# Two attention blocks in one kernel: a two-step projection that may spread over two slots, with a reordered start

## The chip, the cores and the metric

The kernel runs on one core of one Trainium2 chip. The metric is the device time of one execution in microseconds (us), the median of several runs. "Full exponential" below means one ScalarE (ACT) instruction over 128 x 1536 elements.

## The reference

Two multi-head attention blocks, A with full and B with windowed causal attention, each on its own input of 2048 x 512, 32 heads of 16. The results are laid side by side.

```python
def _A_ref(x, wqkv, wo):
    B, S, D = x.shape                      # 1, 2048, 512
    H = 32
    Dh = D // H                            # 16
    qkv = ((x @ wqkv).reshape(B, S, 3, H, Dh)) ...   # to q, k, v by head
    scores = jnp.einsum("bhqd,bhkd->bhqk", q, k) * (Dh ** -0.5)
    p = _softmax(scores, axis=-1)
    o = jnp.einsum("bhqk,bhkd->bhqd", p, v)
    return (... o ...).reshape(B, S, D) @ wo

# _B_ref is the same with W = 256 and, before the softmax:
    mask = (idx[:, None] - idx[None, :] >= 0) & (idx[:, None] - idx[None, :] < W)
    scores = jnp.where(mask[None, None], scores, -1e9)

return jnp.concatenate([a, b], axis=-1)
```

Everything is bf16 at the inputs and the output.

## The kernel before

The kernel is a software pipeline of 731 slots. A slot has three jobs; a job is one head's scores for 128 keys and up to 512 queries. For each slot PE multiplies the scores into three PSUM banks (the tile sps, of which there are two), ACT takes the exponential of all three banks in one instruction (pT), and PE multiplies pT by the values (op). Two slots ahead, the next scores are already being made.

Around this, smaller work is filled in, one step at a time: projections of keys, values and queries and the output product. Each has two steps of two 128x512 products, accumulated in a single bank called ms, which DVE then copies out. A part of the exponentials of block A is not done by ACT but by a polynomial on DVE (steps "d"): one score product into the same bank ms, a copy by DVE, and three DVE operations for every two of them.

Where PE has little else to do in a slot, it multiplies unread products into the scores' bank ahead of the scores; the scores overwrite them. `whole` counts what was filled in during the slot.

```python
    def busy(self, bank, n):
        for _ in range(n):
            self.nc.tensor.matmul(bank, lhsT=self.ident[:], rhs=self.junk, start=True,
                                  stop=True)                                  # line 156

    def scores(self, slot):
        sps = self.ps.tile([P, SLOT, 512], FP32, name="sps", tag="sps", bufs=2)
        for b, jb in enumerate(slot["jobs"]):
            ...
            if b == 0 and jb.inst == 0:                # inst 0 is block A, 1 is block B
                self.busy(sps[:, 0, :], 2 - self.whole)
            for kt, q0, q1, o in jb.subs:
                self.nc.tensor.matmul(sps[:, b, o:o + q1 - q0], ...)          # line 572
        ...                                            # masks of block B, line 581
```

A projection is a pair of steps. The bank is taken in the first and given back in the second:

```python
    def pair(self, first, second):
        def f():
            self.open = self.bank()
            first(self.open[:])                        # products of chunks 0 and 1, line 252
        def g():
            bank, self.open = self.open, None
            self.closed = self.slot
            second(bank[:])                            # chunks 2 and 3, then DVE's copy
        return [f, g]
```

The step of the polynomial, cut to its bank:

```python
        def step(jb):
            ...
            b = self.bank()
            ... nc.tensor.matmul(b[:, o:o + q1 - q0], ...)                    # line 628
            nc.vector.tensor_copy(out=y[:, half, :], in_=b[:])                # line 631
            self.closed = self.last_poly = self.slot   # next one two slots later at best
            ...                                        # three DVE operations, lines 642 to 652
```

A fill is refused when the bank was given back in this very slot, or when DVE would not have freed it:

```python
    def fill(self, s, tasks, done):
        if self.open is None:
            if self.closed == s or not self.by(self.freed, 0.9):
                return False
            self.cur = next((t for t in tasks if t["nb"] <= s and t["after"] <= done
                             and t["ok"]()), None)
            if self.cur is None:
                return False
        t = self.cur
        kind = t["name"][0]
        self.whole += (kind in "kqop") * 2 + (kind in "dv")
        t["steps"].pop(0)()
        ...
```

The loop pays every step from a credit, which grows by the steps that are due per slot:

```python
        for n in range(2):
            self.whole = n - 1
            self.scores(slots[n])
        self.whole = 2
        for s, sl in enumerate(slots):
            self.slot = s
            self.exps(sl)                              # line 599
            ...
            if s + 2 < len(slots):
                self.scores(slots[s + 2])
            ...
            self.values()                              # line 691
            ...
            credit = min(credit + min(self.rate(s, tasks), 2.5), 3.0)
            poly_credit = min(poly_credit + self.rate(s, polys), 3.0)
            self.whole = 0
            ...                                        # a guard product, if the bank is free
            full = s + 2 < len(slots) and all(jb.blocks for jb in slots[s + 2]["jobs"])
            if (poly_credit >= (2.5 if full else 1.0) and self.open is None
                    and self.fill(s, polys, done)):
                poly_credit -= 1.0
            must = self.open is not None
            while ((credit >= (CROWD if full else 1.0) or must)      # CROWD is 3.0
                   and self.fill(s, tasks, done)):
                credit -= 1.0
                must = self.open is not None and not full
                if full:
                    break
```

The start multiplies the first four value tiles, nine heads wide, before the first scores:

```python
        nv = 4
        vb = self.ps.tile([P, SLOT, 512], FP32, name="sps", tag="sps", bufs=2)
        for t in range(nv):
            bank = vb[:, t, :] if t < SLOT else tile_("op", 1)[:]
            self.v_mm(0, t, bank, range(NC), (0, HV))
            self.v_evac(0, t, bank, nc.scalar.copy, (0, HV))
            if t == 0:
                self.pad_guard(0, mq)                  # finishes the first queries, on PE and DVE
```

Of the kernel before, what the change touches and what calls it, by code (L numbers as in the profile page):

```python
# [25 lines left out]
NC = D // P  # L26
NPASS = S // 512
NKT = S // P
SLOT = 3
# [12 lines left out]
HV = 9  # L42
# [72 lines left out]
class _Kernel:  # L115
# [443 lines left out]
# [3 lines that stand above are left out]
            r = slice(32 * jb.j, 32 * jb.j + KR)  # L562
            qT = self.qT[jb.inst, jb.p, jb.g // 2]
            gg = jb.g % 2
            assert jb.key != (0, 0, 1) or self.padq_done
            if b == 0 and jb.inst == 0:

                self.busy(sps[:, 0, :], 2 - self.whole)
            for kt, q0, q1, o in jb.subs:
                kT, k0 = self.kT[jb.inst, jb.g // 2, kt // 4]  # L570
                k0 += (kt % 4) * P
                self.nc.tensor.matmul(sps[:, b, o:o + q1 - q0],  # L572
                                      lhsT=kT[r, gg, k0:k0 + P],
                                      rhs=qT[r, gg, q0:q1], start=(o == jb.subs[0][3]),
                                      stop=not jb.blocks, tile_position=(32 * jb.j, 0),
                                      skip_group_check=True)
        for b, jb in enumerate(slot["jobs"]):
            for kind, o in jb.blocks:
                m = self.mask[:, "fd".index(kind[0]):"fd".index(kind[-1]) + 1, :]
                m = m.rearrange("p a n -> p (a n)")  # L580
                self.nc.tensor.matmul(sps[:, b, o:o + P * len(kind)], lhsT=self.ident[:],  # L581
                                      rhs=m, start=False, stop=True, skip_group_check=True)
        slot["sps"] = sps
# [223 lines left out]
    def start(self):  # L807


        nc = self.nc  # L810
        x = self.t[0]["x"].rearrange("(c k p) d -> p c k d", p=P, k=4)
        xs = [self.tile([P, 2, 4, D], BF16, "kTa", NPAIR) for _ in range(2)]
        load = lambda c, h, eng: eng.dma_start(xs[c // 2][:, c % 2, 2 * h:2 * h + 2],
                                               x[:, c, 2 * h:2 * h + 2])
        load(0, 0, nc.sync)
        load(0, 1, nc.scalar)
        self.load_w(0, 1, nc.sync, (0, P))
        self.load_w(0, 0, nc.scalar, (0, P))
        warm = self.consts.tile([1, 1], FP32, name="warm")
        nc.vector.memset(warm[:], 0.0)  # L820
        nc.scalar.activation(out=warm[:], in_=warm[:], func=ACT.Exp)
        for c in range(1, NPASS):
            for h, eng in enumerate((nc.sync, nc.scalar)):
                load(c, h, eng)
        self.load_w(0, 2, nc.sync)
        self.load_w(0, 1, nc.scalar, (P, D))
        self.load_w(0, 0, nc.sync, (P, D))
        self.constants()
        for gg in range(2):
            for n in (1, 0):  # L830
                self.pad_w(n, gg)
        self.padmax = self.consts.tile([P, 2, NPASS], FP32, name="padmax")
        self.k_begin(0, 0, 0)
        tile_ = lambda tag, bufs: self.ps.tile([P, 512], FP32, name=tag, tag=tag, bufs=bufs)
        big = {}

        def turn(c):
            for h in range(2):
                t = self.ps.tile([P, SLOT, 512], FP32, name="sps", tag="sps", bufs=2)
                tb = big[c, h] = t[:, 0, :].bitcast(BF16).rearrange("p (d n) -> p d n", d=2)  # L840
                for d in range(2):
                    for k in range(4):
                        nc.tensor.transpose(tb[:, d, k * P:(k + 1) * P],
                                            xs[c // 2][:, c % 2, k, (2 * h + d) * P:
                                                       (2 * h + d + 1) * P], self.ident[:])

        def keep(c):
            xT = self.tile([P, NC, 512], BF16, "xT", XRING)
            self.xT[0, c] = xT
            for h in range(2):  # L850
                copy = nc.vector.tensor_copy if h else nc.scalar.copy
                copy(out=xT[:, 2 * h:2 * h + 2, :], in_=big[c, h])

        def keys(c):
            b = self.bank() if c == 2 else tile_("op", 1)
            self.pad_mm(1, 0, c, b[:], range(NC))
            self.pad_k_evac(0, c, b[:])
        for i, n in ((0, NKT), (1, VRING_B)):
            for t in range(n):
                self.v_begin(i, t)  # L860
        b = self.bank()
        for _ in range(36):
            nc.tensor.matmul(b[:, 0:P], lhsT=self.ident[:], rhs=self.ident[:], start=True,
                             stop=True)
        turn(0)
        keep(0)
        turn(1)
        keep(1)
        keys(0)
        b = self.bank()  # L870
        self.pad_mm(0, 0, 0, b[:], range(NC))
        mq = self.pad_q_evac(0, b[:])
        for c in range(2, NPASS):
            turn(c)
            keep(c)
            keys(c - 1)
        keys(NPASS - 1)
        nv = 4
        vb = self.ps.tile([P, SLOT, 512], FP32, name="sps", tag="sps", bufs=2)
        for t in range(nv):  # L880
            bank = vb[:, t, :] if t < SLOT else tile_("op", 1)[:]
            self.v_mm(0, t, bank, range(NC), (0, HV))
            self.v_evac(0, t, bank, nc.scalar.copy, (0, HV))
            if t == 0:
                self.pad_guard(0, mq)
        self.qT[0, 0, 0] = self.padq
        return [("v", 0, t, 0) for t in range(nv)] + [("k", 0, 0), ("q", 0, 0, 0)]

# [127 lines left out]
    def run(self):  # L1016
# [6 lines left out]
        tasks = self.tasks = [t for t in tasks if t["name"][0] != "d"]  # L1023
        credit = poly_credit = 0.0
        for n in range(2):
            self.whole = n - 1
            self.scores(slots[n])
        self.whole = 2
        for s, sl in enumerate(slots):
            self.slot = s  # L1030
            self.exps(sl)
            if s == 2:
                self.more_constants()
                self.load_wo(0)
            if self.dq and self.by(self.vec, 0.6):
                self.queued(1.22, at=0)
                self.dq.pop(0)()
            if s + 2 < len(slots):
                self.scores(slots[s + 2])
            elif s + 1 == len(slots):  # L1040
                self.mid, finish = self.last_out(0, NPASS - 1)
            self.values()
            due = [x for x in self.later if x[0] <= s]
            self.later = [x for x in self.later if x[0] > s]
            for _, f in due:
# [4 lines that stand above are left out]
            if (self.guards and self.guards[0][0] <= s and self.open is None  # L1050
                    and self.by(self.freed, 0.9)):
                self.guards.pop(0)[1]()
                self.closed = s
                self.whole = 1
# [5 lines that stand above are left out]
            while ((credit >= (CROWD if full else 1.0) or must)  # L1060
                   and self.fill(s, tasks, done)):
                credit -= 1.0
                must = self.open is not None and not full
                if full:
                    break
        while self.pend:
# [58 lines left out]
```

## Time and profile before

| | before |
|---|---|
| time, median of 3 runs | 1043.58 us (1042.92 to 1048.24) |
| span of the profiled execution | 1041.2 us |
| ACT busy | 998.4 us, 96% |
| PE busy | 942.3 us, 90% |
| DVE busy | 802.5 us, 77% |
| unread products (line 156) | 735 |
| products of polynomial steps (line 628) | 244 |
| granted clock of PE | 0.999 |

A row of the groups names the line, the engine, what is written from what, the shapes and the count; then the time busy and the mean of one in ns; then how long the engine stood idle just before them, and what ended that. A row of the timeline begins with the start in us from the span's start and the duration; several equal instructions in a row are merged (x4), and the bracket has the idle time before and its releaser. PEld is the load of PE's weights. Records of neighbouring instructions on one engine can overlap, so a pace is better read from start to start than from a duration.

### The profile page before, as it was taken

The numbers are of one execution on the slowest core, as the hardware profiler recorded it, in microseconds if no ns is written. First come the engines' busy times: TensorE is split into PE (matmuls) and PEld (weight loads), VectorE is DVE, ScalarE is ACT, GpSimd is POOL, SyncE is SP. The second block draws the span as 40 slices with busy tenths as digits, with TensorE's granted clock in tenths as the row PEclk, the third lists the DMA queues.
The fourth block names the chain that finished last, engine by engine and source line by source line (L and its number), as shares of the span: only waits on it lengthen the run. The fifth ranks groups of instructions, "written<-read, shape, count | busy, mean of one in ns | idle before, by whom it ended". The sixth has DMA issues, their size and how long they took to land.

```text
span 1041.2 us, 19020 instructions
## 1 busy us (share of the span) xinstructions
PE 942.3 (90%) x7702; PEld 327.3 (31%) x7780; DVE 802.5 (77%) x1032; ACT 998.4 (96%) x763; POOL 20.1 (2%) x100
## 2 busy tenths in 40 slices
PE   7989989999999989999999989899999998899897
PEld 4333222233223323333323333233332333233322
DVE  4533268968978987788888887878888778798974
ACT  5999999999999999999999999999999999999996
POOL 6000000000000000000000000000000000000000
PEclk9999999999999999999999999999999999999999
DMA  7021431212232112211230212123202221221111
GB/s 244 12 76 46 134 109 45 72 63 73 63 88 79 57 35 87 89 58 34 87 99 27 87 62 86 49 79 91 71 21 80 82 79 42 74 73 47 32 33 42
DMA packets 72361, 73.07 MB, mean 70 GB/s; under 512 B 22584, under 2 KB 55888, under 8 KB 72272
## 3 DMA queue, kind: packets, MB, share of 16 engines
q1 hardware_dynamic: 69216, 68.01, 21.5%
q0 software_dynamic: 768, 2.13, 0.5%
q10 hardware_dynamic: 2288, 1.70, 0.5%
q8 instruction: 61, 1.00, 0.4%
q14 instruction: 28, 0.23, 0.1%
HBM read 38.65 MB, written 31.07 MB: 67 GB/s over the span
## 4 chain that ended last, share of the span: by engine, by line
ACT 55%; PE 24%; DVE 11%; issue 8%; DMA 2%; ACTq 0%; DVEq 0%
ACT pT L599 55%; PE ms L252 6%; PE sps L572 5%; PE sps L156 5%; PE op L691 4%; DVE dy L631 3%; PE ms L628 2%; PE sps L581 2%; DVE dh L646 1%; DVE dh L642 1%; DVE pD L652 1%; DMA kTa<-in_A_x_dram 1%; DVE kst L270 1%; DVE osb L772 1%; DVE ob L421 1%
## 5 line engine op out<-in xcount | busy, mean ns | idle before, releaser
L599 ACT ACTIVATE pT<-sps 128x1536 bf16<-128x1536 f32 (+2 forms) x747 | 988.3, 1439 | 23.9 <-PE sps L572 14.4
L156 PE MATMUL sps<-ident 128*128 128x512 bf16 x735 | 239.2, 381 | 49.1 <-ACT pT L599 38.2
L572 PE MATMUL sps<-qTa,kTa 32*128 32x512 bf16 (+1 forms) x1868 | 242.2, 377 | 0.7 <-ACT pT L599 0.7
L631 DVE COPY dy<-ms 128x512 f32<-128x512 f32 x240 | 164.7, 686 | 73.2 <-PE ms L628 69.0
L691 PE MATMUL op<-pT,va 128*32 128x512 bf16 (+1 forms) x1868 | 181.0, 382 | 0.9 <-DVE osb L772 0.8
L642 DVE SCALAR_TENSOR_TENSOR dh<-dy 128x1024 f32<-128x1024 uint16 x120 | 146.1, 1217 | 1.6
L646 DVE SCALAR_TENSOR_TENSOR dh<-dy,dh 128x1024 f32<-128x1024 uint16 x120 | 145.7, 1214 | 1.0
L652 DVE SCALAR_TENSOR_TENSOR pD<-dh,dy 128x1024 uint16<-128x1024 f32 x120 | 145.6, 1213 | 1.0
L572 PEld LDWEIGHTS <-kTa 32*128 32x128 bf16 x1868 | 60.5, 91 | 222.2 <-issue 222.2
L156 PEld LDWEIGHTS <-ident 128*128 128x128 bf16 x735 | 65.2, 96 | 167.7 <-issue 157.0
L628 PE MATMUL ms<-qTa,kTa 32*128 32x512 bf16 (+1 forms) x244 | 91.5, 377 | 9.2 <-DVE ob L421 2.1
L691 PEld LDWEIGHTS <-va 128*32 128x32 bf16 x2112 | 50.0, 93 | 102.4 <-issue 101.1
L581 PE MATMUL sps<-mask,ident 128*128 128x128 bf16 (+1 forms) x640 | 77.8, 248 | 0.0
L572 PE MATMUL sps<-qTb,kTb 32*128 32x384 bf16 (+2 forms) x704 | 58.1, 274 | 13.1 <-ACT pT L599 11.0
L581 PEld LDWEIGHTS <-ident 128*128 128x128 bf16 x640 | 43.4, 97 | 31.7 <-issue 29.3
L772 DVE COPY osb<-op 128x512 f32<-128x512 f32 x62 | 42.5, 685 | 9.6 <-PE op L691 9.5
L270 DVE CAST kst<-ms 128x512 bf16<-128x512 f32 x28 | 19.4, 692 | 31.6 <-PE ms L252 31.0
L345 DVE CAST va<-ms 128x368 bf16<-128x368 f32 (+1 forms) x28 | 11.8, 441 | 37.5 <-PE ms L252 37.4
L376 DVE TENSOR_SCALAR qs<-ms 128x512 bf16<-128x512 f32 x31 | 21.4, 690 | 21.0 <-PE ms L252 20.6
L572 PEld LDWEIGHTS <-kTb 32*128 32x128 bf16 x704 | 25.2, 92 | 37.6 <-issue 33.9
L628 PEld LDWEIGHTS <-kTa 32*128 32x128 bf16 x244 | 22.0, 91 | 46.4 <-issue 45.5
L691 PE MATMUL op<-pT,vb 128*32 128x384 bf16 (+2 forms) x704 | 36.0, 280 | 0.3 <-DVE osb L772 0.3
(106 smaller groups left out, 445.9 us busy)
## 6 DMA issues: line engine op xcount, KB each, us to landing
od<-osb SPq DMA_DIRECT2D x62, 256.0 KB
oc<-od SPq DMA_DIRECT2D x31, 256.0 KB
rb<-rd SPq DMA_DIRECT2D x31, 256.0 KB
kTb<-kd SPq DMA_DIRECT2D x16, 256.0 KB
qTb<-qd SPq DMA_DIRECT2D x16, 256.0 KB
qd<-qs SPq DMA_DIRECT2D x31, 128.0 KB
out_dram<-ob SPq DMA_DIRECT2D x31, 128.0 KB
qTa<-qd SPq DMA_DIRECT2D x15, 256.0 KB
```

Source lines behind the costliest of these rows:

```text
L156: self.nc.tensor.matmul(bank, lhsT=self.ident[:], rhs=self.junk, start=True, stop=True)
L252: self.nc.tensor.matmul(bank, lhsT=lhs(c), rhs=rhs(c), start=(c == 0), stop=(c == NC - 1))
L572: self.nc.tensor.matmul(sps[:, b, o:o + q1 - q0], lhsT=kT[r, gg, k0:k0 + P], rhs=qT[r, gg, q0:q1], start=(o == jb.subs[0][3]), stop=not jb ...
L581: self.nc.tensor.matmul(sps[:, b, o:o + P * len(kind)], lhsT=self.ident[:], rhs=m, start=False, stop=True, skip_group_check=True)
L599: nc.scalar.activation(out=pT[:, b:e, :n], in_=sps[:, b:e, :n], func=ACT.Exp, scale=LN2 / 128, bias=-127 * LN2)
L628: nc.tensor.matmul(b[:, o:o + q1 - q0], lhsT=kT[r, g % 2, k0:k0 + P], rhs=self.qT[0, p, g // 2][r, g % 2, q0:q1], start=True, stop=True, t ...
L631: nc.vector.tensor_copy(out=y[:, half, :], in_=b[:])
L642: nc.vector.scalar_tensor_tensor(out=st["h"][:], in0=low, scalar=-65536.0, in1=low, op0=ALU.add, op1=ALU.mult)
L646: nc.vector.scalar_tensor_tensor(out=st["h"][:], in0=low, scalar=65536.0 * POLY[1], in1=st["h"][:], op0=ALU.add, op1=ALU.mult)
L652: nc.vector.scalar_tensor_tensor(out=out.bitcast(U16), in0=st["h"][:], scalar=POLY[0] * 2.0 ** -41, in1=flat, op0=ALU.mult, op1=ALU.add)
L691: self.nc.tensor.matmul(op[32 * jb.j:32 * jb.j + 32, q0:q1], lhsT=self.v[jb.inst, kt][:, h * VP:h * VP + 32], rhs=jb.pT[:, o:o + q1 - q0], ...
L772: nc.vector.tensor_copy(out=osb[:], in_=self.op[i, p, g][:])
```

## The change

It has four parts. In the loop, the second step of a pair is no longer forced into the slot of the first: `must` is false after a fill, and the pair is finished in the next slot, unless the credit alone pays for both. Slots that begin with block B but also hold jobs of block A now get an unread product too, one at most. The first two slots get none and one unread products in place of three and two. At the start the four value tiles are multiplied in a row, and copied afterwards, two by ACT and two by DVE. The aim is to spread PE's work evenly over slots and to shorten the start.

```diff
-            if b == 0 and jb.inst == 0:
-
-                self.busy(sps[:, 0, :], 2 - self.whole)
+            if b == 0 and any(x.inst == 0 for x in slot["jobs"]):
+
+                self.busy(sps[:, 0, :], (2 if jb.inst == 0 else 1) - self.whole)
...
+        banks = [vb[:, t, :] if t < SLOT else tile_("op", 1)[:] for t in range(nv)]
         for t in range(nv):
-            bank = vb[:, t, :] if t < SLOT else tile_("op", 1)[:]
-            self.v_mm(0, t, bank, range(NC), (0, HV))
-            self.v_evac(0, t, bank, nc.scalar.copy, (0, HV))
+            self.v_mm(0, t, banks[t], range(NC), (0, HV))
             if t == 0:
                 self.pad_guard(0, mq)
+        for t in range(nv):
+            self.v_evac(0, t, banks[t], nc.scalar.copy if t < 2 else nc.vector.tensor_copy,
+                        (0, HV))
...
         for n in range(2):
-            self.whole = n - 1
+            self.whole = 2 - n
             self.scores(slots[n])
...
                 credit -= 1.0
-                must = self.open is not None and not full
+                must = False
```

## The prediction

> **What bounds the kernel now.** I read the shares of busy time first, then the groups of instructions, the waits of ACT, and the timeline of single slots. A slot is one step of the kernel's main loop: one exponential over three banks (1536 columns) and the products around it.
>
> ```profile
> PE 942.3 (90%) x7702; PEld 327.3 (31%) x7780; DVE 802.5 (77%) x1032; ACT 998.4 (96%) x763; POOL 20.1 (2%) x100
> ...
> L599 ACT ACTIVATE pT<-sps 128x1536 bf16<-128x1536 f32 x705 | 962.6, 1481 | 23.2 <-PE sps L572 14.2 <-PE sps L581 4.3 <-PE op L691 1.4
> L156 PE MATMUL sps<-ident 128*128 128x512 bf16 x735 | 239.2, 381 | 49.1 <-ACT pT L599 38.2
> ```
>
> ACT is the bound, and 735 of PE's products are unread ones (line 156), 2 in a slot that has nothing else to do. PE's 90% therefore hides room. The idle 23.2 us before the exponential understates what a better feed could give, because records overlap by up to 0.15 us: consecutive exponentials that wait for nothing start 1.330 us apart though one lasts 1.481. So I went through the starts of the 705 full exponentials in the trace. Their mean distance is 1.393 us, more than half stand within 10 ns of 1.330, and the excess over 1.330 is 705 x 0.063 = 44.6 us (47.1 us with the shorter exponentials of the windowed instance). That is all a better feed can win in the loop.
>
> For each late exponential I then looked at what PE did between the scores before and the scores it waited for:
>
> - four projection products (line 252), i.e. both steps of a projection in one slot: 126 such slots, 88 late, 26.4 us in all, 0.30 us each;
> - a product for the polynomial on DVE (line 628) in the slot right after such a slot: 40 late, 6.5 us; other line 628 slots: 39 late, some 8 us;
> - two unread products: 251 such slots, about 7 of them late;
> - the rest, some 4 us, is scattered or at the start.
>
> The timeline shows one of the first kind:
>
> ```profile
> 325.16 1.02 PE L252 MATMUL ms<-wo,oTa 128*128 128x512 bf16 x4 [0.33 <-DVE dy L631]
> ...
> 326.11 0.39 PE L572 MATMUL sps<-qTa,kTa 32*128 32x512 bf16 x3
> 326.22 0.69 DVE L421 CAST ob<-ms 128x512 bf16<-128x512 f32 x1 [1.11 <-PE ms L252]
> ...
> 326.61 2.92 ACT L599 ACTIVATE pT<-sps 128x1536 bf16<-128x1536 f32 x2 [0.51 <-PE sps L572]
> ...
> 326.96 0.37 PE L628 MATMUL ms<-qTa,kTa 32*128 32x512 bf16 x1 [0.23 <-DVE ob L421]
> ...
> 328.11 0.59 PE L156 MATMUL sps<-ident 128*128 128x512 bf16 x2
> 328.64 0.39 PE L572 MATMUL sps<-qTa,kTa 32*128 32x512 bf16 x3
> ```
>
> The four products hold the scores back to 326.11, ACT idles 0.51 us for them, and the next line 628 product then waits 0.23 us for the bank that DVE is still copying. Two slots later two unread products take 0.53 us from start to the scores, and nobody waits.
>
> **What the Trainium skill says.** "TensorE: Matmul & The Clock Gate", section "Wait — 56ns, not 53.3ns?", has warm 512-column products start 215.7 ns apart. The trace agrees: 215 ns within line 156 and within line 252 alike. So two projection products cost PE exactly what two unread ones cost; this carries the prediction. "ScalarE: Activation LUTs", section "What ACT_TABLE_LOAD costs", says back-to-back ACTIVATEs overlap by some 93 ns; here it is 1481 - 1330 = 151 ns, and I use the measured 1.330 as floor. "PSUM — Partial Sum Buffer", section "PSUM bank collisions raise a hardware error", says that two engines must not touch one bank at once; at the start the kernel goes further and waits although the value tiles lie in different banks, as the trace shows below.
>
> **Part 1: the loop no longer forces the second step.** With must = False, a projection's first step (two products) stays in its slot, and the second comes in the next. In PE's cycle from fill to fill: scores 0.33, values 0.33, then the fill and the unread products before the next scores. Before: four products, 0.95 us from the first to the next scores (325.16 to 326.11), together 1.61 us against ACT's 1.33; 0.28 short, close to the measured mean of 0.30. After: two products and no unread one (whole is 2), 0.53, together 1.19, as in a slot of two unread products. So a split slot should be on time.
>
> Not every pair is split. The while loop goes on by itself if the credit was 2 or more at the first step. I worked the kernel's own bookkeeping through its 731 slots (it depends on slot numbers only): 35 of 126 first steps find a credit of 2 or more, often the cap of 3.0 after a stretch of windowed slots; 91 find less. Matched in order with the slots of the trace, the 90 that would split carry 20.4 us of excess and 4.0 us of the line 628 waits after them; those that stay carry 5.9 and 1.7. **Term: -24.4 us.** About 2 x 90 = 180 unread products go too, from 735 to some 560; they are not on the bound's path.
>
> **Part 2: what the split gives back.** The one bank ms is now held over two slots. A polynomial product needs it free, and there are 240; they come two slots apart at best, so a pair between two of them used to be free and now delays the second by a slot. Demand is 240 x 2 + some 70 split pairs after slot 60 = 550 of 670 slots: it fits, but polynomials will come later and credits be higher, so some more pairs find a credit of 2. I take 2 us. Of the waits that a first step has for DVE's copy of the slot before (the waits view: line 252 on DVE L631, 4.4 us in 14 waits) most stay, and slots with eight value products (0.55 instead of 0.33, total 1.41) stay slightly late: 3.5 us. **Term: +5.5.**
>
> **Part 3: mixed slots.** Of the 32 slots with both instances, 16 begin with the windowed one; only these gain an unread product, and only where the slot before filled nothing. At most 16 x 0.215 = 3.4 us, of which most falls in PE's waiting time. **Term: +0.7.**
>
> **Part 4: the start.**
>
> ```profile
> 18.69 0.41 PE L252 MATMUL sps<-wv,xT 128*128 128x144 bf16 x4
> ...
> 19.14 0.28 ACT L345 CAST va<-sps 128x144 bf16<-128x144 f32 x1 [0.50 <-PE sps L252]
> 19.47 0.41 PE L252 MATMUL sps<-wv,xT 128*128 128x144 bf16 x4 [0.37 <-ACT va L345]
> ...
> 19.97 0.81 PE L156 MATMUL sps<-ident 128*128 128x512 bf16 x3
> ...
> 20.71 0.39 PE L572 MATMUL sps<-qTa,kTa 32*128 32x512 bf16 x3
> ...
> 21.15 19.27 ACT L599 ACTIVATE pT<-sps 128x1536 bf16<-128x1536 f32 x14 [0.70 <-PE sps L572]
> ```
>
> Value tile and copy alternate: each tile waits for the copy of the one before. In a row, tiles 1 to 3 take 0.25 us each (19.47 to 19.72 here), so PE is done at 18.69 + 0.75 = 19.44. Three unread products (0.74 us to the scores) go from the first slot, and one of two from the second. The scores then wait for the padded queries, which DVE finishes at 19.54: scores at about 19.6, first exponential at about 20.05 instead of 21.15. ACT's two copies (0.25 us apart) end by about 19.95, DVE's two by 20.1, in time for the second slot. The rest of the loop follows ACT, so the gain stays. **Term: -1.1.**
>
> **Sum.** 1043.6 - 24.4 + 5.5 + 0.7 - 1.1 = 1024.3; I say 1024.
>
> **Rivals.** (a) The bank becomes the new bound. If polynomials fall behind, a head group's last value products wait for them, the six pT buffers fill, and ACT stops. For it: rows of polynomial products every second slot, already at their closest. Against it: they fall due 13 slots ahead of the head group's end. It would eat most of the gain or more: 1035 to 1050. (b) The excess only moves: DVE, 77% busy with operations of 1.2 us, copies each bank as late as before, and the first step waits for it. The 4.4 us of that wait speak against much of this; it would make 1028 to 1034. (c) Credits drift up, since a blocked first step keeps collecting; then half of the pairs stay whole and the gain is 14 us: 1030. (d) PE's slack lets the other late line 628 slots recover too (8 us), and giving back is near nothing: 1015.
>
> **Range and chances.** Low is (d), 1016; high takes (b) and (c) together, 1034. The 2% line is 1022.7, just under my number: faster 0.40, within 2% 0.56, slower 0.04 (only (a) at its worst).
>
> **What would show it.** Right: line 156 down to some 560; slots with four line 252 products down from 126 to about 40 and slots with two up to about 180; full exponentials 1.36 us apart on average; the first at about 20.05; ACT's wait for line 572 cut by half or more. Wrong: slots of two projection products that are late by more than 0.1 us on average; waits of line 252 for DVE grown well over 4.4 us; ACT waiting for line 691; polynomial products bunched and exponentials stopped for a slot or more; a first exponential still near 21.

## The result, and the profile after

The changed kernel takes 1028.31 us (median of 4 runs, 1026.73 to 1031.01) against 1043.90 us. The ratio is 0.9845, with a 95% interval from 0.9809 to 0.9882: a gain of about 16 us, clear of noise and just under 2%.

The page after, the same rows as before (name, shapes and count, then busy us and mean ns, then the idle time before and its releasers):

```profile
span 1027.7 us, 18738 instructions
...
PE 920.7 (90%) x7583; PEld 314.2 (31%) x7664; DVE 804.5 (78%) x1034; ACT 994.3 (97%) x761; POOL 20.0 (2%) x100
...
PEclk8999999999999999999999999999999999999999
...
L156 PE MATMUL sps<-ident 128*128 128x512 bf16 x619 | 209.7, 382 | 48.9 <-ACT pT L599 41.1
```

And the group of the full exponentials:

```profile
L599 ACT ACTIVATE pT<-sps 128x1536 bf16<-128x1536 f32 x705 | 958.7, 1503 | 14.0 <-PE sps L572 8.9 <-PE sps L581 2.5 <-PE op L691 0.3
```

ACT's idle time before the full exponentials fell from 23.2 to 14.0 us, and 116 unread products are gone. From start to start, the 705 exponentials are now 1.374 us apart on average instead of 1.393; the excess over the 1.330 of unhindered ones fell from 44.6 to 31.3 us. Read slot by slot, as for the prediction (with the windowed instance's shorter exponentials), the lateness went this way. What is counted are the 746 exponentials after the first; a slot whose jobs differ in width has two.

| slot filled with | before: count, of these late, us lost | changed: count, of these late, us lost |
|---|---|---|
| a whole pair (four products of line 252) | 126, 88, 26.4 | 37, 27, 7.8 |
| half a pair (two) | 8, 4, 1.3 | 186, 40, 8.1 |
| a polynomial product (line 628) | 275, 79, 14.1 | 281, 71, 14.2 |
| a guard product or nothing | 337, 15, 5.3 | 242, 18, 4.8 |
| sum | 47.1 | 35.0 |

So 18.6 us left the whole pairs, 6.8 came back in the halves, and the polynomial's slots gained nothing. The slice row PEclk shows something new: the first slice has an 8. PE ran at half clock from 19.65 to 26.48 us, and again for 3.4 us at 255.

Two things have to be known to read the table. Six slots in each column of the first row are not pairs: they hold value tiles whose eight narrow products go in one step. By the kernel's own bookkeeping (some products have no record in a trace) 124 of 126 pairs were finished in one slot before, and 32 are now. And some 3 us of the 35.0 lie in the two stretches of half clock: about 1.8 in four of those value tiles, just after the start, and 1.2 in one half at 257 us. At full clock, then, some 20.4 us left the first row and 5.6 came back in the halves.

At the start the chain is shorter, as planned:

```profile
18.65 0.41 PE L252 MATMUL op<-wv,xT 128*128 128x144 bf16 x4
...
18.85 0.46 ACT L345 CAST va<-sps 128x144 bf16<-128x144 f32 x2 [0.82 <-PE sps L252]
...
19.15 0.39 PE L572 MATMUL sps<-qTa,kTa 32*128 32x512 bf16 x3
...
19.35 0.31 DVE L345 CAST va<-sps 128x144 bf16<-128x144 f32 x1 [0.25 <-ACT va L345]
...
19.59 5.66 ACT L599 ACTIVATE pT<-sps 128x1536 bf16<-128x1536 f32 x4 [0.28 <-PE sps L572]
...
20.23 0.61 PE L572 MATMUL sps<-qTa,kTa 32*128 32x512 bf16 x3
```

The value tiles follow one another without waiting for copies, and the first exponential starts at 19.59 instead of 21.15 us; 0.44 us of that is an earlier finish of the padded queries in this execution (19.10 instead of 19.54). From 20.23 on the same scores take 0.61 us instead of 0.39: that is the half clock.

### The profile page after: what moved, and what is told of

Same layout as the page of the kernel before. It is cut to its first block, busy times and chain, and to the rows that moved or that the text cites. A ratio compares the mean times of both kernels' runs of the same rounds, so it can differ in the third digit from the quotient of the medians.

```text
span 1027.7 us, 18738 instructions
## 1 busy us (share of the span) xinstructions
PE 920.7 (90%) x7583; PEld 314.2 (31%) x7664; DVE 804.5 (78%) x1034; ACT 994.3 (97%) x761; POOL 20.0 (2%) x100
## 4 chain that ended last, share of the span: by engine, by line
ACT 53%; PE 22%; DVE 13%; issue 10%; DMA 2%; ACTq 0%; DVEq 0%
ACT pT L599 53%; PE sps L572 5%; PE ms L252 5%; PE op L691 4%; PE sps L156 4%; DVE dy L631 3%; DVE dh L642 3%; DVE dh L646 2%; PE sps L581 2%; PE ms L628 2%; DVE pD L652 1%; DMA kTa<-in_A_x_dram 1%; DVE ob L421 1%; DMA wk<-in_B_wqkv_dram 1%; DVE osb L772 1%
## 5 line engine op out<-in xcount | busy, mean ns | idle before, releaser
L156 PE MATMUL sps<-ident 128*128 128x512 bf16 x619 | 209.7, 382 | 48.9 <-ACT pT L599 41.1
L631 DVE COPY dy<-ms 128x512 f32<-128x512 f32 x240 | 164.3, 685 | 64.3 <-PE ms L628 62.5
L156 PEld LDWEIGHTS <-ident 128*128 128x128 bf16 x619 | 57.3, 96 | 160.4 <-issue 149.6
L581 PEld LDWEIGHTS <-ident 128*128 128x128 bf16 x640 | 43.4, 97 | 32.1 <-issue 29.5
L252 PE MATMUL ms<-wv,xT 128*128 128x368 bf16 (+2 forms) x163 | 36.1, 322 | 3.4 <-DVE dy L631 1.7
L252 PE MATMUL ms<-xT,wq 128*128 128x512 bf16 x100 | 32.3, 389 | 3.7 <-DVE dy L631 1.5
```

The lines of the kernel that those rows point to most:

```text
L252: self.nc.tensor.matmul(bank, lhsT=lhs(c), rhs=rhs(c), start=(c == 0), stop=(c == NC - 1))
```

## The experiments

**How times are compared.** Each run has a granted PE clock, from 0.988 to 1.000 in the runs of the kernel before, and the time follows it: within the kernels of this study, 0.001 less clock goes with 0.75 us more. Besides the ratio of the times as they ran, I give the time "at full clock", each run reduced by that slope and then averaged, with a 95% interval: the kernel before 1042.4 ± 0.2 us, the changed one 1025.8 ± 0.9. It is a fit, used only to separate effects of 1 or 2 us from the clock. The kernels did not all run on one chip; on each of the four that ran the experiments the kernel before comes to 1042.2 to 1042.6 at full clock.

| kernel | ratio to before, 95% | mean clock | at full clock, us |
|---|---|---|---|
| before (83 runs) | 1 | 0.995 | 1042.4 ± 0.2 |
| changed | 0.9845 (0.9809 to 0.9882) | 0.996 | 1025.8 ± 0.9 |
| split alone | 0.9843 (0.9816 to 0.9871) | 0.994 | 1026.0 ± 0.2 |
| start alone | 1.0013 (0.9992 to 1.0034) | 0.991 | 1041.3 ± 0.5 |
| mixed slots alone | 1.0034 (1.0013 to 1.0055) | 0.992 | 1044.1 ± 0.3 |
| changed, unread products of the start back | 0.9840 (0.9812 to 0.9867) | 0.996 | 1027.1 ± 0.3 |
| changed, more pairs split | 0.9802 (0.9776 to 0.9828) | 0.998 | 1024.1 ± 0.4 |
| changed, no unread products | 1.0577 (1.0528 to 1.0626) | 0.768 | too far to reduce |
| changed, none beside a polynomial product | 0.9988 (0.9963 to 1.0013) | 0.964 | 1018.6, an extrapolation |
| changed, no mixed slots | 0.9820 (0.9794 to 0.9846) | 0.997 | 1025.5 ± 0.5 |
| before, block B's keys later | 0.9986 (0.9973 to 1.0000) | 0.997 | 1042.3 ± 0.3 |
| more split, keys later, no mixed slots | 0.9808 (0.9782 to 0.9835) | 0.995 | 1021.9 ± 0.4 |
| changed, one DVE operation of three | 0.9755 (0.9721 to 0.9788) | 0.999 | 1019.4 ± 0.3 |
| more split, keys later, mixed slots | 0.9791 (0.9767 to 0.9815) | 0.997 | 1023.7 ± 0.4 |

For the kernel with none beside a polynomial product, two of 14 runs, over 1.5% above its fastest, are left out.

### Which part carries the gain

The split alone, on the kernel before:

```diff
-                must = self.open is not None and not full
+                must = False
```

> The kernel before with only the forced second step taken out. Theory A (the split carries the gain): 12 us less than before, ratio 0.988, with about 37 whole pairs and 90 split ones as in the changed kernel, and PE's granted clock at 1.00. Theory B (the reordered start and the mixed slots carry a good part): 6 us less or fewer, ratio 0.994 or more.

Ratio 0.9843: the split is the whole gain, 16.4 us at full clock, more than the 12 expected. Its trace has 37 slots with a whole pair as the table counts them, and a lateness of 32.9 us in place of 47.1. The clock was not at 1.00 but at 0.994 on average, about that of the kernel before (0.995). Theory A stands, B falls. That it also has 122 unread products fewer is not the reason: the slots that held a whole pair, and were late, had none before.

The start alone: value tiles in a row, ACT and DVE copying, and

```diff
-            self.whole = n - 1
+            self.whole = 2 - n
```

> The kernel before with only the start changed (value tiles in a row, two copiers, none and one unread products). Theory A: the first exponential 1.5 us earlier as in the changed kernel (19.6 instead of 21.15), the whole 1.5 us shorter, ratio 0.9985. Theory C (fewer unread products at the start cost PE's clock): a stretch of half clock of about 7 us after the first scores in some runs, as in the profiled run of the changed kernel at 19.65; such a run keeps little or nothing of the 1.5 us.

The first exponential starts 0.49 us after DVE has finished the padded queries (19.26, then 19.75), where it took 1.61 before (19.54, then 21.15): 1.1 us shorter, and at full clock so is the kernel. As it ran it won nothing (1.0013, interval across 1): its clock was lower on average, 0.991 against 0.995. But its profiled half stretch lay at 154 us, not after the first scores. Nor do the other profiles tie the half clock to the new start: of the seven kernels that have it, and their other unread products, two show a stretch at 20 us (the changed one and the one without mixed slots), of the five with the old start one does (block B's keys later).

The mixed slots alone:

```diff
-            if b == 0 and jb.inst == 0:
-                self.busy(sps[:, 0, :], 2 - self.whole)
+            if b == 0 and any(x.inst == 0 for x in slot["jobs"]):
+                self.busy(sps[:, 0, :], (2 if jb.inst == 0 else 1) - self.whole)
```

> The kernel before with only the unread product in the 16 slots that begin with block B and hold block A too. Theory A: at most 16 more products of 0.215 us, most of them in PE's waiting time: 0 to 1 us longer, ratio 1.000 to 1.001. Theory C (such products keep the clock): no gain, since the kernel before had its clock at 0.999.

Slower: 1.0034 as it ran, 1.7 us at full clock, for 12 more unread products (747 instead of 735). That is 0.14 us for each of them on average. The expectation of 0 to 1 us was too low. Its profile also shows what can stand before half clock:

```profile
PEclk9999998999999999999999999999999999899999
```

and in PE's timeline, just before the stretch that begins at 154.9 us:

```profile
151.44 0.39 PE L572 MATMUL sps<-qTa,kTa 32*128 32x512 bf16 x3
153.76 1.04 PE L252 MATMUL ms<-xT,wk 128*128 128x512 bf16 x4 [1.93 <-DMA wk<-in_B_wqkv_dram]
154.73 0.46 PE L572 MATMUL sps<-qTa,kTa 32*128 32x512 bf16 x3
155.11 0.62 PE L691 MATMUL op<-pT,va 128*32 128x512 bf16 x4
```

PE stood still for 1.93 us, for the key weights of block B. In the 3.41 us before the half stretch PE was 43% busy; the products afterwards take 0.62 instead of 0.40. The start alone had the same picture at 153.75 (56% busy before), and the changed kernel at 19.65 (51%, after PE's 1.46 us wait for the queries' guard). But the profiled execution of the kernel before waited for the same weights, and kept its clock (0.999 on average, no half stretch in the loop):

```profile
152.75 1.04 PE L252 MATMUL ms<-xT,wk 128*128 128x512 bf16 x3 [1.41 <-DMA wk<-in_B_wqkv_dram]
```

So such a wait can be followed by half clock, and need not be.

The unread products of the first two slots put back into the changed kernel (`self.whole = n - 1`):

> The changed kernel with the three and two unread products of the first two slots put back. Theory A: the first exponential later by no more than the three products, 0.6 to 0.7 us, and the same 0.6 to 0.7 us more in all. Theory C (their absence costs the clock): no half clock after the first scores, every run at 0.999 or more, and a median 1 to 3 us below the changed kernel's 1028.3 in spite of the later start.

The first exponential starts 0.98 us after the padded queries, 0.49 later than in the changed kernel. The five runs had a clock of 0.993 to 0.999, the changed kernel's four 0.992 to 1.000, with the same mean, and at full clock it is 1.3 ± 1.0 us longer. So those products cost what theory A says or somewhat more, and no gain in clock shows: theory C finds no support here, and the lower clock of the start alone stays unexplained.

### Unread products and the clock

None at all in the changed kernel (`range(n)` made `range(0)`):

> The changed kernel with none of its 619 unread products. Theory C (they keep PE's clock): the granted clock falls well below 0.99, to 0.9 or less, and the time rises above 1060 us. Rival (they only take PE's time; the clock's half stretches come from PE's waits alone): clock 0.99 or more and 1015 us or less, since every score then comes up to 0.43 us earlier.

1103.61 us. The slices of the clock, of ACT and of PE:

```profile
PE   7887788979888889888988888888987888888887
...
ACT  5999989998898989998898899999899998999995
...
PEclk8999878586668865887587898788587986786758
```

PE falls to half clock 47 times; 0.77 on average. The unread products are not idle work: together they are worth 75 us here.

One step of it: a slot with a polynomial product gets none instead of one.

```diff
-        self.whole += (kind in "kqop") * 2 + (kind in "dv")
+        self.whole += (kind in "kqopd") * 2 + (kind in "v")
```

> The changed kernel where a slot with a product for the polynomial gets no unread product at all instead of one: 431 of them instead of 619. Theory P (these slots are late because PE's cycle is full: 0.33 + 0.33 + 0.64 = 1.30 us of 1.33, and 1.52 with eight value products): their lateness falls from 14 us to 5, the time by 8 us at the same clock. Rival Q (they are late because the bank is still being copied): the lateness stays above 11 us. Theory C: the clock falls below 0.99 and takes some of it back.

Both happen. At full clock it would be 1018.6, 7.2 us less, so these slots are late in part because PE's cycle is full; the size is an extrapolation over 0.036 of clock. But the clock fell to 0.964, and as it runs it is at 0.9988 of the kernel before: it lost all of the change's gain. The lateness by slot kind can't be read here, for the half stretches lie in it.

Block B's key projections on the kernel before, held back until the weights have landed:

```diff
+        self.w_at[i, n] = self.slot                       # in load_w
...
+                     ok=lambda: self.slot >= self.w_at[1, 1] + 6)   # for tasks ("k", 1, ...)
```

> The kernel before where block B's key projections start no sooner than six slots after their weights were asked for; nothing else is changed. Theory C (the half clock at 154 us follows from PE standing still for these weights, 1.8 us in the profiled run of the kernel with mixed slots alone): no stretch of half clock between 150 and 165 us, the granted clock 0.997 or more on average instead of 0.995, and 1 to 3 us less than the kernel before. Rival (the half stretches come at any place with a short wait of PE, by the phase of the clock's watch): the one at 154 us is only moved, and clock and time stay as they are.

Over 22 runs the clock was 0.997 instead of 0.995, the time 1.3 us lower on average than in the 27 runs of the kernel before on the same chip, the ratio 0.9986 with an interval that touches 1; at full clock nothing changed. So what it gains, if anything, comes with the clock, as theory C says. Its profile has no stretch near 154 us, but neither has that of the kernel before; other stretches remain (19.9 and 880.1 us).

### What is left of the lateness

More pairs split, by a higher bar for finishing in the same slot:

```diff
-                if full:
+                if full or self.open is not None and credit < 1.99:
                     break
```

> The changed kernel where a pair is finished in its own slot only if its first step found the full credit of 3.0: by the kernel's bookkeeping 17 whole pairs and 109 split ones instead of 32 and 94. Theory A (a whole pair costs ACT 0.21 us, a split one 0.09, as the two traces of the changed kernel's slots show): 2 us less at the same granted clock. Rival (the bank, held longer, now holds back the polynomial's products): as much is lost in the slots of line 628, and the time stays the same or rises.

1.7 us less at full clock, close to the 2 expected; whole pairs fell to 2.3 us of lateness, halves stayed at 8.6. As it ran it had the lowest median of the study's complete kernels, 1024.72 us.

Is the rest DVE? Here its first two operations of every polynomial are left out (the third works on the raw scores, so a part of the attention weights is another; everything else is as in the changed kernel):

```diff
             def first():
-                st["h"] = ...
-                nc.vector.scalar_tensor_tensor(out=st["h"][:], in0=low, scalar=-65536.0, ...)
+                pass
             def second():
-                nc.vector.scalar_tensor_tensor(out=st["h"][:], in0=low, ...)
+                pass
```

> The changed kernel with the first two of DVE's three operations of the polynomial left out (the third works on the scores alone, so the weights of these keys are not those of the reference); the order of all other work is the same. Theory Q (what is left of the lateness comes from DVE, which copies the bank late): line 252's wait for DVE's copy falls from 7.5 to below 3 us, the first steps after a polynomial product lose their 4 us of lateness, line 628 slots fall from 14 to 7, and the time by 8 us or more at equal clock. Rival P (PE's cycle is full in these slots): the waits fall, the lateness and the time hardly do, under 3 us.

At full clock 6.4 us less. Line 252's wait for DVE's copy (L631), 7.5 us in the changed kernel, is gone from the longest waits; ACT's waits are these:

```profile
ACT pT L599 <- PE sps L572: 3.5, 13, 0.6
ACT pT L599 <- PE sps L581: 1.9, 9, 0.4
ACT pT L599 <- PE op L687: 0.8, 2, 0.5
```

(us in total, times, longest.) The first halves that follow a polynomial product fell from 4.1 to 1.6 us of lateness. The first row of the table fell from 7.8 to 4.7, but 1.8 of that is the half clock of the changed kernel's profile, which this one doesn't have. The line 628 slots fell only from 14.2 to 11.4, where theory Q wanted 7. So both theories hold, for different slots: DVE's late copy for the first halves; for the polynomial's own slots DVE's part is small, and PE's full cycle is the likelier cause, by the 7.2 us of the kernel that has no unread product there. The changed kernel's timeline shows the first case:

```profile
327.10 1.21 DVE L652 SCALAR_TENSOR_TENSOR pD<-dh,dy 128x1024 uint16<-128x1024 f32 x1
...
327.25 0.38 PE L628 MATMUL ms<-qTa,kTa 32*128 32x512 bf16 x1
...
328.42 0.69 DVE L631 COPY dy<-ms 128x512 f32<-128x512 f32 x1
...
329.16 0.59 PE L252 MATMUL ms<-xT,wq 128*128 128x512 bf16 x2 [0.56 <-DVE dy L631]
...
329.68 0.39 PE L572 MATMUL sps<-qTa,kTa 32*128 32x512 bf16 x3
...
330.18 2.79 ACT L599 ACTIVATE pT<-sps 128x1536 bf16<-128x1536 f32 x2 [0.22 <-PE sps L572]
330.34 0.61 PE L252 MATMUL ms<-xT,wq 128*128 128x512 bf16 x2
330.88 0.39 PE L572 MATMUL sps<-qTa,kTa 32*128 32x512 bf16 x3
```

The polynomial product is done at 327.63, but DVE is at an operation of 1.21 us until 328.31; its copy frees the bank at 329.11, the first half starts 0.56 us late at 329.16, and ACT loses 0.22. The second half at 330.34 has the bank already and costs nothing.

### Putting parts together

> The changed kernel without the unread product in the mixed slots (10 of the 16 slots get one). Theory A, from the single parts at equal clock (split -16.5, start -1.3, mixed +1.6 us): 1.6 us less than the changed kernel, ratio to the kernel before 0.983. Rival C (the product keeps the clock through the window's slots): more half clock, and the same time or more.

The changed kernel without the mixed slots' products: 0.3 ± 1 us less at full clock. Too close to tell 1.6 from nothing, because the changed kernel itself has four runs only.

> The kernel with 17 whole and 109 split pairs, without the unread product in the mixed slots and with block B's keys six slots after their weights. Theory A: at equal clock 1024.1 less up to 1.6 for the mixed slots, and with the clock at 0.998 or more 1023 to 1025 us as it runs, ratio to the kernel before 0.979. Rival: the parts don't add, and it stays at the 0.980 of the kernel with more split pairs.

More split, keys later, no mixed products: 1021.9 at full clock, the lowest of the complete kernels that ran near it. As it ran, with a clock of 0.995, it was at 0.9808, no better than more split alone.

> The kernel with 17 whole and 109 split pairs and block B's keys six slots after their weights, with the unread product of the mixed slots kept. Theory C (that product holds the clock: the same kernel without it ran at 0.9946 on average, the one with it and without later keys at 0.998): the granted clock back at 0.998 and 1023 to 1024 us as it runs. Rival (the clock of five runs varies by chance, and the product only costs its time): the clock anywhere between 0.994 and 0.998, and at equal clock 0 to 2 us more than the 1022.0 of the kernel without it.

The same with the mixed products: clock 0.997, and 1.8 us more at full clock. The rival holds: these products cost their time, as in the kernel before (1.7), and five runs don't show that they hold the clock. All three variants with more split pairs are about 2% faster than the kernel before (0.979 to 0.981), and as they ran they can't be ranked.

## Why the prediction came out as it did

The time lay 4 us above the 1024 predicted, inside the range, and within 2% as the likeliest of the three classes had it. The prediction's terms are -18.9 for the split, +0.7 for the mixed slots and -1.1 for the start, -19.3 in all. Measured one by one at full clock they are -16.4, +1.7 and -1.1, together -15.8; measured in one kernel, -16.6 ± 0.9. So the mechanism was right, and the two terms of cost, what the split gives back and the mixed slots, were too small.

- **Part 1, the split.** Mechanism and count were right: slots with four or more products of line 252 fell from 126 to 37 (some 40 predicted), half slots rose to 186 (some 180), and the lateness of the former fell by 18.6 us in the profile, by some 20.4 without the half clock, where 20.4 was predicted. The rest of the term, 4.0 us of waits of line 628 after a whole pair, did not come: the lateness behind whole pairs did fall, from 5.7 to 2.4 us, but as much appeared behind halves and guards, and the line 628 slots as a whole stayed at 14.
- **Part 2, what it gives back.** This is the mis-sized term. The split was worth 24.4 - 5.5 = 18.9 on paper and 16.4 measured by itself. The halves' lateness rose by 6.8 us (5.6 without the half clock) where 3.5 stood for all that stays late: line 252's waits for the copy did not stay at 4.4 us in 14 waits but rose to 7.5 in 18. It isn't that more first steps come one slot behind a polynomial product: by the kernel's bookkeeping 76 did before, and 74 do now. Why they wait longer is not shown; that DVE's operations make them wait is, for without two of the three this wait was gone.
- **Unread products.** Predicted some 560, found 619. Value projections count one per step in `whole`, so a split value pair keeps an unread product in each slot; the working took two away for every pair.
- **Part 3, mixed slots.** +0.7 was too small: 1.7 to 1.8 us in two of three comparisons. The assumption that they fall mostly into PE's waiting time was wrong.
- **Part 4, the start.** -1.1 predicted, -1.1 by itself at full clock. The first exponential came at 19.59; with the 0.44 us by which the queries were earlier in that execution, 20.03 against 20.05.
- **Rivals.** (a) did not happen; ACT's wait for line 691 stayed under 1 us. (b) is the one that did in part: DVE's occupation is 6.4 us of what is left. (c) did not: 32 whole pairs by the bookkeeping, where 35 first steps had the credit before. (d) failed, as line 628 slots did not recover.
- **Signs.** Full exponentials are 1.374 us apart, not 1.36, and ACT's wait for line 572 fell from 14.4 to 8.9 us, less than the half or more expected; both say that part 2 was too small. What the working had left out altogether is the clock, which spreads the runs of one kernel over 9 us.

## What to carry to other kernels

Two projection products where two unread ones stood cost PE nothing more; four in one slot made the bound engine late in 88 of 126 cases, by 0.30 us each. So before sizing a fill, write PE's cycle from scores to scores and compare it with the bound engine's pace. When work is spread, look at what holds the shared bank in the slot before: here DVE's queue accounts for 6.4 us of what is left. And before removing filler products, measure the clock that they buy.

## What the runs showed of the hardware

PE's clock is not lost only after long idleness. In the profiles of kernels that ran near full clock, PE falls to half clock for 3.4, 6.8 or 10.2 us at a time, multiples of 3.41. Of 13 such stretches inside the loop or at its start, six followed 3.41 us in which PE was, by its records, still 43 to 57% busy. Five of these six stood behind a single wait of 1.46 to 1.93 us; yet the kernel before had waits of 1.47 and 1.41 us in the same two places and kept full clock. "TensorE: Matmul & The Clock Gate", section "What's actually happening", gives the same window of 3413 ns and calls it free-running, which fits that one execution falls into half clock where another doesn't; it speaks of an idle window, and here a half-busy one was enough. Not explained are the other seven stretches, that at 255 us of the changed kernel among them: the 3.41 us before them were 72 to 88% busy.
